# The first load of all on the second DMA queue: k's first head pair issued by ScalarE beside q's first half on SyncE

## The chip, the cores and the metric

One core of a Trainium2 chip. The metric is the device time of one execution in microseconds (us); the median of several executions is quoted. The profile's span, from the first to the last instruction, is some 1.8 us shorter than the time and is used for comparing traces. Runs are compared only with the other kernel's runs from the same rounds on the same chip.

## The reference, cut to what matters

```python
# q, k, v: (8 batches, 8 heads, 576 positions, 64), float32
q_s = softmax(q, axis=-1); k_s = softmax(k, axis=2)
kv  = einsum('bhsd,bhse->bhde', k_s, v)
x   = einsum('bhsd,bhde->bhse', q_s, kv)     # -> (4608 tokens, 512)
h   = x @ w_in                               # w_in (512, 2048)
out = gelu(h) @ w_out                        # w_out (2048, 512), float32
```

## The kernel before

All inputs come in over SyncE's DMA queue, in the order in which the front of the kernel uses them. ScalarE's queue only sends four "touches", loads of 16 x 2 numbers, one from each tensor that is read later. The parts that the argument needs:

```python
    def load_main(b, name, t, parts=1):        # q: 128 partitions x 8 heads
        ...
        for i in range(parts):
            nc.sync.dma_start(out=f[:, i * n:(i + 1) * n, :], in_=src[:, i * n:(i + 1) * n, :])

    def load_pair(b, name, t, parts=1):        # k, v: 128 partitions x 4 head pairs
        ...
        for i in range(parts):
            nc.sync.dma_start(out=f[:, i * n:(i + 1) * n, :], in_=src[:, i * n:(i + 1) * n, :])
    ...
    touch = singles.tile([16, 4, 2], FP32)
    for i, a in enumerate((k[0]..., v[0]..., moe_w_in[0:128:8, 0:2], moe_w_out[0:512:32, 0:2])):
        nc.scalar.dma_start(out=touch[:, i, :], in_=a)

    load_main(0, "q", q, 2)                    # two halves, 524 KB each
    load_pair(0, "k", k, 2)                    # two halves, 590 KB each
    load_pair(0, "v", v, 4)
    wi = [load_wi(i) for i in range(5)]        # w_in in five column blocks
    wo = [load_wo(i) for i in range(3)]
    ...
    exp_q(0, parts=2); exp_k(0, parts=2)       # ScalarE
    norm_q(0, 0, 2)                            # sum on VectorE, product on GpSimd
    norm_q(0, 1, 2, nc.vector)
    tp_mm(0, 0); tp_evac(0, 0, "s")            # transposes of q, copy on ScalarE
    ...
    cast_wi(0, wi[0], "p"); cast_wi(1, wi[1], "p")   # first weight blocks, GpSimd
    ...
    h_phase(0, {...})                          # 64 matmuls with w_in: "the phase"
```

Below, "the phase" is this first matmul phase, and "the gate" is the wait in its middle for w_in's fourth column block.

The softmax here doesn't subtract the row's maximum and nothing guards it: scores larger than these inputs give would overflow.

## Time and profile before

| | before |
|---|---|
| time, median of 3 first runs (range) | 280.57 us (280.5 to 281.31) |
| profiled run: time, span | 280.69, 278.9 us |
| the phase starts | 14.57 us |
| the gate: last piece of w_in's fourth block lands | 21.67 us |
| from the phase's end on | tensor engine without a break |

The prediction shows the chain of waits, the weight loads and the transfers. Some more lines of the kernel before will be needed. The first four are from the timelines by engine (start us, length us, instruction, in brackets the idle time before it and who ended it): q's first exp on ScalarE, GpSimd's casts of v and of the first weight block, and the last weight loads of the tensor engine before the phase, for the small matmuls that multiply q by k.v (kvc).

```profile
4.43 2.62 ACT L133 ACTIVATE e<-f 128x512 bf16<-128x512 f32 x6 [0.30 <-DMA f<-in_q_dram]
...
10.96 2.15 POOL L145 CAST v_aug<-f 128x576 bf16<-128x576 f32 x3 [1.69 <-DMA f<-in_v_dram]
...
13.78 2.59 POOL L378 CAST wi_bf<-w 128x512 bf16<-128x512 f32 x4 [0.68 <-DMA w<-in_moe_w_in_dram]
...
14.23 0.11 PEld L254 LDWEIGHTS <-kvc 64*64 64x64 bf16 x4 [0.71 <-DVE kvc L177]
```

The phase's first weight load at 14.57 comes 0.34 us after the last group of kvc loads begins, at 14.23. The view in the prediction names the weight cast on GpSimd as what ended its wait of 0.23 us. That is an inference from the last signal before it: the first part of that cast had ended at 14.43, and the same 0.34 and 0.23 us stand in the changed kernel, where no cast is named. So the phase did not wait for the weights here; it followed the k.v work, and that waited for GpSimd's last cast of v (end at 13.11, the next k.v weight load at 13.16). The other lines are stretches of the front (from:to, length, busy time of each engine, then clock, DMA share, GB/s):

```profile
1.80:2.80 1.00, 1.00 (x2) 0.48 (x2) 0.14 (x2) 0.17 (x1) 0.00 (x0) 1.00 0.59 151
2.80:5.00 2.20, 2.20 (x3) 0.68 (x3) 0.00 (x0) 1.89 (x4) 0.00 (x0) 1.00 1.09 379
5.00:6.00 1.00, 1.00 (x3) 0.46 (x2) 0.30 (x1) 0.86 (x4) 0.00 (x0) 1.00 1.00 303
6.00:8.00 2.00, 2.00 (x5) 0.87 (x4) 1.97 (x3) 1.05 (x3) 0.64 (x1) 1.00 1.04 366
```

The last column shows the ramp (151) and the dip at the change from q to k (303).

### The profile page before, as it was taken

Reading aid. Unit: us, or ns where it says so; the run is one execution under the profiler, and the core shown is the slowest. Engines: PE = TensorE matmul, PEld = TensorE weight load, DVE = VectorE, ACT = ScalarE, POOL = GpSimd, SP = SyncE. Lnnn points to the kernel's source line nnn. Section 1 sums busy time; section 2 is a strip of 40 time slices with the busy share of each in tenths; the row PEclk is TensorE's granted clock in tenths of the full one; section 3 lists DMA queues with packets and bytes.
Section 4 is the critical chain, followed back from the end, with each engine's and each line's share of the span. In section 5 each row is a group of like instructions: output and inputs, shape, how many; then the busy total and the mean of one; then the engine's idle time right before and its main releaser. Section 6 shows DMA issues by size and latency. Waiting matters only on the chain.

```text
span 278.9 us, 4564 instructions
## 1 busy us (share of the span) xinstructions
PE 272.2 (98%) x1922; PEld 125.8 (45%) x1922; DVE 102.1 (37%) x152; ACT 157.0 (56%) x243; POOL 33.0 (12%) x25
## 2 busy tenths in 40 slices
PE   7899999999999999999999999999999999999995
PEld 3343454444444444444444444444444444444443
DVE  3767486309753530093007500651015200130012
ACT  5747665689377816691569346943683263036400
POOL 1530050002020130004000500050005000000000
PEclk9999999999999999999999999999999999999999
DMA  7999999962993139812981189117501500120033
GB/s 237 385 405 428 399 401 407 399 257 74 305 352 64 41 109 240 329 38 73 256 349 41 40 219 384 49 66 185 119 0 75 150 2 0 75 78 0 0 78 76
DMA packets 44996, 50.10 MB, mean 180 GB/s; under 512 B 20400, under 2 KB 29872, under 8 KB 44720
## 3 DMA queue, kind: packets, MB, share of 16 engines
q1 hardware_dynamic: 44688, 49.68, 53.3%
q8 instruction: 15, 0.25, 0.3%
q10 hardware_dynamic: 288, 0.13, 0.2%
q14 instruction: 5, 0.04, 0.1%
HBM read 36.70 MB, written 9.44 MB: 165 GB/s over the span
## 4 chain that ended last, share of the span: by engine, by line
PE 91%; DMA 7%; DVE 1%; ACTq 0%; issue 0%
PE ps L308 44%; PE ps L298 42%; DMA w<-in_moe_w_in_dram 3%; DMA f<-in_v_dram 2%; PE kv L166 2%; DMA touch<-in_moe_w_in_dram 2%; PE ps L254 1%; PE ps L330 1%; DVE wi_bf L381 0%; ACTq L433 0%; PE ps L259 0%; PE ps L215 0%; PE tp L215 0%; DVE y_sb L335 0%; PE xx L254 0%
## 5 line engine op out<-in xcount | busy, mean ns | idle before, releaser
L298 PE MATMUL ps<-xT,wi_bf 128*128 128x512 bf16 x576 | 126.4, 379 | 0.3
L308 PE MATMUL ps<-wo_bf,g 128*128 128x512 bf16 x560 | 124.2, 379 | 0.0
L303 ACT ACTIVATE g<-ps 128x512 bf16<-128x512 f32 x144 | 85.2, 597 | 69.3 <-PE ps L298 69.3
L298 PEld LDWEIGHTS <-wi_bf 128*128 128x128 bf16 x576 | 56.2, 98 | 68.9 <-DVE wi_bf L381 1.0
L308 PEld LDWEIGHTS <-g 128*128 128x128 bf16 x560 | 53.9, 98 | 64.6 <-issue 0.8
L315 DVE COPY y_sb<-ps 128x512 f32<-128x512 f32 x35 | 23.9, 686 | 81.4 <-PE ps L308 81.1
L198 POOL TENSOR_TENSOR e<-e,recq 128x2048 bf16<-128x2048 bf16 (+1 forms) x9 | 25.7, 2856 | 178.1 <-DVE recq L197 150.0
L145 DVE CAST v_aug<-f 128x576 bf16<-128x576 f32 x26 | 17.9, 745 | 46.9 <-DMA f<-in_v_dram 46.9
L196 DVE TENSOR_REDUCE qsum<-e 128x16 f32<-128x1024 bf16 (+1 forms) x13 | 21.0, 1615 | 13.9 <-ACT e L133 13.9
L280 ACT CAST xT<-ps 128x512 bf16<-128x512 f32 x19 | 10.3, 589 | 26.7 <-PE ps L254 17.1
L133 ACT ACTIVATE e<-f 128x512 bf16<-128x512 f32 (+1 forms) x42 | 20.5, 556 | 2.4 <-DMA f<-in_q_dram 2.0
L138 ACT ACTIVATE ek<-f 128x2304 bf16<-128x2304 f32 (+1 forms) x10 | 17.2, 1730 | 1.8 <-DMA f<-in_k_dram 1.8
L278 DVE CAST xT<-ps 128x512 bf16<-128x512 f32 x15 | 9.7, 687 | 17.5 <-PE ps L254 14.6
L79 ACT ACT_TABLE_LOAD x9 | 11.5, 1283 | 2.8 <-issue 2.6
L415 PE MATMUL ps<-zeros 128*128 128x512 f32 (+1 forms) x14 | 8.6, 764 | 1.5 <-DVE zeros L447 1.5
L133 ACT ACT_TABLE_LOAD x7 | 9.0, 1283 | 0.1
L381 DVE CAST wi_bf<-w 128x512 bf16<-128x512 f32 x12 | 7.4, 661 | 2.6 <-DMA w<-in_moe_w_in_dram 2.3
L166 PEld LDWEIGHTS <-ek 64*64 64x64 bf16 x576 | 6.3, 105 | 2.6 <-issue 1.1
L166 PE MATMUL kv<-v_aug,ek 64*64 64x65 bf16 x576 | 6.9, 193 | 0.0
L198 DVE TENSOR_TENSOR e<-e,recq 128x1024 bf16<-128x1024 bf16 x4 | 6.4, 1606 | 0.1
L254 PE MATMUL ps<-qT,kvc 64*64 64x512 bf16 x60 | 5.0, 390 | 1.0 <-DVE kvc L177 1.0
L408 DVE CAST wo_bf<-w 128x2048 bf16<-128x2048 f32 (+1 forms) x4 | 4.4, 1090 | 3.9 <-DMA w<-in_moe_w_out_dram 3.9
(35 smaller groups left out, 42.8 us busy)
## 6 DMA issues: line engine op xcount, KB each, us to landing
out_dram<-y_sb SPq DMA_DIRECT2D x32, 256.0 KB, 2.3
f<-in_k_dram SPq DMA_DIRECT2D x6, 1152.0 KB, 10.0
f<-in_v_dram SPq DMA_DIRECT2D x6, 1152.0 KB, 11.7
f<-in_q_dram SPq DMA_DIRECT2D x6, 1024.0 KB, 7.1
w<-in_moe_w_in_dram SPq DMA_DIRECT2D x6, 512.0 KB, 8.9
f<-in_k_dram SPq DMA_DIRECT2D x4, 576.0 KB, 10.0
f<-in_v_dram SPq DMA_DIRECT2D x8, 288.0 KB, 7.8
f<-in_q_dram SPq DMA_DIRECT2D x4, 512.0 KB, 8.5
```

What stands on the lines that cost most here:

```text
L79: nc.scalar.activation(out=scr[:, 1:2], in_=scr[:, 0:1], func=func)
L133: nc.scalar.activation(out=dst[:, i], in_=src[:, u], func=AF.Exp)
L138: nc.scalar.activation(out=ek[b % 2][:, i:i + n], in_=st[b]["kf"][:, i:i + n].rearrange("p x (n d) -> p x n d", n=NS), func=AF.Exp,)
L145: eng.tensor_copy(out=v_aug[b % 2][:, hp, :, 0:D], in_=st[b]["vf"][:, hp, :].rearrange("p (n d) -> p n d", n=NS),)
L166: nc.tensor.matmul(ps[c, i, half, 0:D + 1], ek[b % 2][pr, hp, n, :], v_aug[b % 2][pr, hp, n, 0:D + 1], start=(n == 0), stop=(n == NS - 1),)
L196: nc.vector.reduce_sum(out=qsum, in_=eq[:, :, hs, :], axis=AX.X)
L198: eng.tensor_tensor(out=eq[:, :, hs, :], in0=eq[:, :, hs, :], in1=recq.unsqueeze(3).to_broadcast([128, J, w, D]), op=ALU.mult,)
L280: nc.scalar.copy(out=st[b]["xT"][:, hp, :], in_=ps)
L298: nc.tensor.matmul(ps, wi_bf[:, dm, t * 128:(t + 1) * 128], xT[:, dm, :], start=(dm == 0), stop=(dm == NDM - 1),)
L303: nc.scalar.activation(out=g[:, t, :], in_=ps, func=AF.Gelu)
L308: nc.tensor.matmul(ps, st[c]["g"][:, t, j * 128:(j + 1) * 128], wo_bf[:, t, :], start=(t == 0), stop=(t == NDF - 1),)
L315: nc.vector.tensor_copy(out=y_sb, in_=ps)
```

## The change

The intent: no data move before about 1.8 us and the transfers then start slowly, on one queue. k's first head pair (295 KB) goes onto ScalarE's idle queue, in the slot of the touch of k, so that two queues feed the engines from the start. The other touches stay.

```diff
         for i in range(parts):
-            nc.sync.dma_start(out=f[:, i * n:(i + 1) * n, :], in_=src[:, i * n:(i + 1) * n, :])
+            h0 = i * n
+            if b == 0 and name == "k" and i == 0:
+                nc.scalar.dma_start(out=f[:, 0, :], in_=src[:, 0, :])
+                h0 = 1
+            nc.sync.dma_start(out=f[:, h0:(i + 1) * n, :], in_=src[:, h0:(i + 1) * n, :])
...
+    load_main(0, "q", q, 2)
+    load_pair(0, "k", k, 2)
-    touch = singles.tile([16, 4, 2], FP32)
-    for i, a in enumerate((k[0]..., v[0]..., moe_w_in..., moe_w_out...)):
+    touch = singles.tile([16, 3, 2], FP32)
+    for i, a in enumerate((v[0]..., moe_w_in..., moe_w_out...)):
         nc.scalar.dma_start(out=touch[:, i, :], in_=a)
-    load_main(0, "q", q, 2)
-    load_pair(0, "k", k, 2)
```

More of the change, by code (lines that the diff above doesn't have):

```diff
@@ L425, in warm_x @@
                 )
-    touch = singles.tile([16, 4, 2], FP32)
-    for i, a in enumerate((k[0].rearrange("h (p n) d -> (h p) (n d)", n=NS)[0:128:8, 0:2],
-                           v[0].rearrange("h (p n) d -> (h p) (n d)", n=NS)[0:128:8, 0:2],
+    load_main(0, "q", q, 2)
+    load_pair(0, "k", k, 2)
+    touch = singles.tile([16, 3, 2], FP32)
+    for i, a in enumerate((v[0].rearrange("h (p n) d -> (h p) (n d)", n=NS)[0:128:8, 0:2],
                            moe_w_in[0:128:8, 0:2], moe_w_out[0:512:32, 0:2])):
         nc.scalar.dma_start(out=touch[:, i, :], in_=a)
-    load_main(0, "q", q, 2)
-    load_pair(0, "k", k, 2)
     load_pair(0, "v", v, 4)
```

## The prediction

> **What bounds the kernel now.** I read four views of the kernel before, in this order: the page (who is busy), the chain of waits in order of time for the first 60 us (what sets the end), the transfers from 1.2 to 9.2 us in forty slices (what the first loads do), and the timeline of the first 31 us by engine (who waits for which load).
>
> The page first: engine busy times, then the shares of the chain that ended last.
>
> ```profile
> span 278.9 us, 4564 instructions
> PE 272.2 (98%) x1922; PEld 125.8 (45%) x1922; DVE 102.1 (37%) x152; ACT 157.0 (56%) x243; POOL 33.0 (12%) x25
> ...
> PE 91%; DMA 7%; DVE 1%; ACTq 0%; issue 0%
> ```
>
> The tensor engine is the bound. Only 7% of the chain, some 20 us, is transfers, and they are all at the start. So a change to the first load can act on that part alone. The chain there, in order of time (start us, length us, what):
>
> ```profile
> 1.68 4.27 DMA touch<-in_moe_w_in_dram
> ...
> 5.97 6.41 DMA f<-in_v_dram
> ...
> 12.40 9.27 DMA w<-in_moe_w_in_dram
> ...
> 21.69 1.16 DVE wi_bf L381 x2
> 22.89 6.43 PE ps L298 x29
> 29.33 10.36 PE ps L308 x48
> ```
>
> The last transfer on the chain is a piece of the first weight (its fourth block, columns 1024 to 1535, second half). It lands at 12.40 + 9.27 = 21.67 us. Two VectorE casts take it to 22.85, and from 22.89 the tensor engine follows without a break that matters: 48 matmuls in 10.36 us is 0.216 us each. Before that it had started the big matmul phase at 14.57 us. The phase has 64 matmuls, so 64 x 0.216 = 13.8 us of work, and it ends at 29.33: about 0.9 us lie idle in it by the chain. The timeline of the weight loads says where (start, length, what, the wait before and its releaser):
>
> ```profile
> 14.57 4.00 PEld L298 LDWEIGHTS <-wi_bf 128*128 128x128 bf16 x20 [0.23 <-POOL wi_bf L378]
> ...
> 22.36 0.10 PEld L298 LDWEIGHTS <-wi_bf 128*128 128x128 bf16 x1 [0.58 <-DVE wi_bf L381]
> 22.89 5.94 PEld L298 LDWEIGHTS <-wi_bf 128*128 128x128 bf16 x29 [0.43 <-DVE wi_bf L381]
> ```
>
> By 22.36 it has done 34 matmuls, 14.57 + 34 x 0.216 = 21.91; it resumes fully at 22.89 after the 35th. So the loss at this gate is about 22.89 - 21.91 - 0.22 = 0.76 us. That is the model I use: the end moves with the later of two lines, A = start of the phase + 13.8, B = landing of that weight piece + casts + 29 matmuls. Today B is later by about 0.76 us.
>
> What sets that landing? The transfers from 1.2 us on, each slice 0.2 us:
>
> ```profile
> DMA  0003735999999999999998879999999899899999
> GB/s 0 0 0 52 82 113 195 312 374 394 374 364 374 364 374 404 379 364 399 331 339 292 265 288 369 369 357 380 369 380 380 311 346 403 334 357 369 415 392 438
> ```
>
> From 2.8 us the 16 DMA engines are full, and by the slices of the whole page they stay so to beyond 40 us. Each weight piece lies some 9 us in the queue, so its landing is (bytes ahead) / (rate) + (when the stream got going). Only the last is open to this change. Two holes are to be had. The ramp from 1.8 to 2.8 us: the five slices are short of 374 by 322 + 292 + 261 + 179 + 62 = 1116, x 0.2 us = 223 KB, or 0.60 us at 374 GB/s. The dip where q gives way to k (5.0 to 6.0 us): 43 + 35 + 82 + 109 + 86 = 355, x 0.2 = 71 KB, or 0.19 us. Nothing moves before 1.8 us though the first issue is at 0.73, and the change can't help that. So the most that can be won is about 0.8 us, 0.3% of the span.
>
> **What the Trainium skill says.** "DMA: Bandwidth & Descriptors", section "Issuing engines are not separate DMA queues": DMAs started from ScalarE and SyncE run on the same 16 engines and interleave, and a second issuer saves only the sequencer's time. The trace agrees on the steady part: 0.9 to 1.0 busy from 2.8 us with one issuer. Only the ramp, 0.1 to 0.7 busy, leaves anything. Same page, "Queues, rings and completion order": each DMA engine takes turns between queues at packet granularity, a packet being some descriptors. The four tiny touches on ScalarE's queue show a coarse turn here: issued 0.46 us apart (0.74, 1.22, 1.68, 2.16), they land 2.2, 3.3, 4.3 and 5.4 us later, that is at 2.9, 4.5, 6.0 and 7.6, 1.5 us apart. A half of q, 524 KB at 374 GB/s, is 1.4 us. So it looks as if each touch waits for about one whole transfer of the other queue. Same page, "Specifications": a first byte takes about 0.6 us from the sync/scalar path. Here the first packets come at 1.8, 1.1 us after the first issue; the measurement decides.
>
> **The change, part by part.**
>
> Removed: the touch of k, 0.44 us of ScalarE's queue and a few bytes. In its slot ScalarE issues k's first head pair, 128 x 576 floats = 295 KB. One issue costs about as much (0.33 to 0.65 us for the like-shaped v pieces), so the three other touches, the table load (2.63) and the first exp keep their places: zero to +0.2 us, and that exp waits for q anyway.
>
> Moved: SyncE loads k's second head pair alone, so it has one issue more, about 0.4 us. The queue is six microseconds deep there; not on the path. Total bytes are unchanged.
>
> The ramp: two queues now feed the engines from 1.8 us. If the slow start is each queue's own (its first descriptors and first reads), the second stream fills the engines while the first is still slow: up to 0.60 us of the ramp. If it is a slowness of the engines or the memory, nothing. The touch of k did get its 28 packets through by 2.2 us beside q, so the second queue can be served then. I take 0.3 us, half the ramp: my choice, not a reading. For the dip at k I take a quarter, 0.05 us, as k's tensor is now in use before. Sum: landings about 0.35 us earlier all along.
>
> q's cost: 295 KB now compete with q's first half. At 374 GB/s that is 0.79 us, less the 0.3 filled: q's first half lands up to 0.5 us later (4.4 to 4.9), its second half too if the pair is served ahead of it. ScalarE's six exps (4.43 to 7.05) and VectorE's unbroken run from 5.70 (sum, reciprocal, sum, reciprocal, product, cast of v until 11.01) slip by up to 0.5. But k.v needs also the second v cast, on GpSimd, which waits for v until 10.96 and ends at 11.63: 0.6 us of slack against VectorE's 11.01. The transposes of q's second half, ahead of it in the tensor engine's order, slip from 10.5 to about 11.0. So A starts 0 to 0.3 us later (14.57 to 14.87 at worst), while v's and the weights' earlier landings pull the other way. A has 0.76 of slack.
>
> k's first exp needs both head pairs of its half, thus the same bytes as before: 8.05 becomes about 7.7.
>
> Result: B gains 0.35, A is no hindrance: 280.57 - 0.35 = 280.2 us.
>
> **The rivals.**
>
> One, no gain (280.5): the engines serve q's descriptors first and the pair just stands in line, so the ramp stays as it was. For it: the coarse turns seen with the touches, and the skill's sentence on issuers. Against: the early packets of k's touch.
>
> Two, the semaphores bite (280.8 to 281.5). Each load waits for the one eight places before it: v's first piece waited for the touch of k, landed at 2.9, and was issued at 2.98. It now waits for the 295 KB pair, some 4 to 5 us. The touches lie behind the pair, so v's third and fourth pieces and the second weight block, which wait for them, are issued up to 1 us later, at about 6, 7 and 8.5 us. Does the stream run dry? q and k are 2.2 MB; with 0.15 MB gone by 2.8 us they last to 2.8 + 2.05 / 0.374 = 8.3 us, and v's first pieces are then issued since 5. The stock holds. A later touch could also fail to do whatever it was put there for; the touch of v at 5 to 6.5 still precedes v's first packets at about 8.
>
> Three, the late q wins over the early weights (+0.2): it needs A to slip by more than 0.76 us, more than the 0.5 that bytes can give.
>
> Four, the full ramp and dip are won: -0.8, 279.8.
>
> **Range and chances.** Centre 280.2. The three runs before lie at 280.5, 280.57 and 281.31, so chance alone moves a median by a few tenths. From rival four to a no-gain run with some bad luck: 279.7 to 280.9. A 2% change is 5.6 us; the holes hold 0.8 us, and the losses that I can think of under 2. So 1% faster, 98% same, 1% slower.
>
> **What would show it.** Right: slices from 1.8 to 2.8 us nearer to full; 0.3 MB on the second queue there; q's first exp up to 0.5 us later than 4.43; the weight gate at about 21.3 in place of 21.67, and VectorE waits before the weight loads down from 1.0 to some 0.7 us; from there on the same tensor engine work. Wrong: the ramp as before (rival one); DMA slices under 0.9 between 6 and 10 us, or the chain of waits going through a late touch to a late v (rival two); weight loads running unbroken at 22 us but starting much later than 14.57 (rival three).

## The result, and the profile after

The changed kernel takes 280.46 us (median of 6 runs, 280.38 to 280.63); the kernel before took 280.53 in the same rounds (6 runs, 280.42 to 281.31). The ratio is 0.9992, 95% interval 0.9979 to 1.0005: the same. (A ratio is the mean time of one kernel's runs over that of the other's in the same rounds, so not quite the ratio of the medians.) What differs more is the scatter: 0.25 us after, 0.9 us before.

The page of the changed kernel, span and shares of the chain:

```profile
span 278.6 us, 4537 instructions
...
PE 93%; DMA 2%; ACT 1%; issue 1%; DVE 1%; POOL 1%; POOLq 0%
```

Transfers fell from 7% of the chain to 2%, and the span only from 278.9 to 278.6. So something else has taken their place. The chain of waits of the changed kernel, in order of time, names it:

```profile
0.73 4.34 DMA f<-in_q_dram
...
5.10 1.25 ACT e L138 x3
...
6.37 1.23 DVE qsum L201
...
8.03 1.91 POOL e L203
...
11.68 1.28 ACT L79
...
15.38 3.83 PE ps L303 x17
19.25 7.07 PE ps L303 x32
```

No weight is on it any more. It begins with the load of q, which lands at 0.73 + 4.34 = 5.07, and goes through the exp and the sum, later through the small matmuls of k.v and of q with k.v, to the start of the phase. Then the matmuls run through. Its steps from GpSimd's product to the table load (L79) are again inferred, and the last of them is not a wait: in the kernel before, the matmul that is said to follow it began at 12.75, with the table's first use only ending at 13.10. What carries q's delay on is VectorE, which ends the product of q's second half at 11.02, 0.67 us later than before (10.35); the table at the end of the experiments tests that. Weight loads of the tensor engine, to be laid beside those of before:

```profile
14.93 4.00 PEld L303 LDWEIGHTS <-wi_bf 128*128 128x128 bf16 x20 [0.23 <-issue]
19.25 9.38 PEld L303 LDWEIGHTS <-wi_bf 128*128 128x128 bf16 x44 [0.32 <-issue]
```

The waits of 0.58 and 0.43 us at the gate are gone (the block's last piece now lands at 20.94, 0.74 us earlier), and 44 loads run in one piece. But the phase starts at 14.93 in place of 14.57. The timelines say why (ScalarE, VectorE's product, GpSimd's casts, the last kvc loads):

```profile
5.10 1.24 ACT L138 ACTIVATE e<-f 128x512 bf16<-128x512 f32 x3 [0.97 <-DMA f<-in_q_dram]
6.66 1.24 ACT L138 ACTIVATE e<-f 128x512 bf16<-128x512 f32 x3 [0.32 <-DMA f<-in_q_dram]
...
9.47 1.54 DVE L203 TENSOR_TENSOR e<-e,recq 128x1024 bf16<-128x1024 bf16 x1
...
10.35 2.40 POOL L150 CAST v_aug<-f 128x576 bf16<-128x576 f32 x3 [0.42 <-DMA f<-in_v_dram]
...
13.16 2.58 POOL L383 CAST wi_bf<-w 128x512 bf16<-128x512 f32 x4 [0.40 <-DMA w<-in_moe_w_in_dram]
...
14.59 0.11 PEld L259 LDWEIGHTS <-kvc 64*64 64x64 bf16 x4 [0.73 <-DVE kvc L182]
```

GpSimd's last cast of v ends 0.35 us earlier (12.76, was 13.11), and the first weight block is cast 0.62 us earlier (13.16, was 13.78), but q's first exp comes 0.67 us later (5.10, was 4.43). The net of the two traces, counted at the next phase's first weight load: 28.95 before, 28.74 after, 0.2 us, and that difference is still there at the end. The stretches of the front, changed kernel:

```profile
1.80:2.80 1.00, 1.00 (x2) 0.48 (x2) 0.13 (x2) 0.17 (x1) 0.00 (x0) 1.00 0.91 238
2.80:5.00 2.20, 2.20 (x3) 0.68 (x3) 0.00 (x0) 1.31 (x2) 0.00 (x0) 1.00 1.02 351
5.00:6.00 1.00, 1.00 (x3) 0.53 (x2) 0.00 (x0) 0.90 (x3) 0.00 (x0) 1.00 1.07 376
6.00:8.00 2.00, 2.00 (x5) 0.57 (x3) 1.54 (x3) 1.68 (x6) 0.00 (x0) 1.00 1.05 407
```

The same as forty slices of 0.2 us from 1.2 to 9.2 us, to be laid beside the row in the prediction:

```profile
DMA  0006993977999999999999999999999999999999
GB/s 0 0 0 219 300 224 108 339 246 278 371 364 389 394 384 364 359 364 353 384 369 358 376 392 397 403 369 415 403 438 403 392 415 438 415 369 403 438 426 392
```

The ramp is uneven now (DMA 0.91 busy, yet at 238 GB/s), and from 3.2 us no dip is left. In the ramp 87 KB more were moved, but by 5 us 62 KB of them were given back (351 for 379 GB/s, over 2.2 us): 25 KB, or 0.07 us. The gain came later: 73 KB in the dip, 82 KB from 6 to 8 us, together 155 KB, or 0.41 us at 374 GB/s.

### The profile page after: what moved, and what is told of

It reads as the page before. It is cut to its first block, busy times and chain, and to the rows that moved or that the text cites. A ratio compares the mean times of both kernels' runs of the same rounds, so it can differ in the third digit from the quotient of the medians.

```text
span 278.6 us, 4537 instructions
## 1 busy us (share of the span) xinstructions
PE 268.5 (96%) x1894; PEld 125.5 (45%) x1922; DVE 101.7 (36%) x152; ACT 156.7 (56%) x243; POOL 33.2 (12%) x25
## 4 chain that ended last, share of the span: by engine, by line
PE 93%; DMA 2%; ACT 1%; issue 1%; DVE 1%; POOL 1%; POOLq 0%
PE ps L303 45%; PE ps L313 43%; PE kv L171 2%; PE ps L259 2%; DMA f<-in_q_dram 2%; PE ps L335 1%; POOL e L203 1%; ACT L79 0%; ACT e L138 0%; DVE qsum L201 0%; PE ps L220 0%; ACT qT L231 0%; PE ps L264 0%; PE tp L220 0%; DVE kvc L182 0%
## 5 line engine op out<-in xcount | busy, mean ns | idle before, releaser
L313 PE MATMUL ps<-wo_bf,g 128*128 128x512 bf16 x542 | 122.1, 379 | 1.7 <-issue 1.1
L420 PE MATMUL ps<-zeros 128*128 128x512 f32 (+1 forms) x14 | 7.8, 698 | 1.4 <-DVE zeros L451 1.4
```

What stands on the lines that cost most here:

```text
L313: nc.tensor.matmul(ps, st[c]["g"][:, t, j * 128:(j + 1) * 128], wo_bf[:, t, :], start=(t == 0), stop=(t == NDF - 1),)
```

## The experiments

Theory at the outset: the phase starts with the later of two arrivals, q's or the first weights', and runs on with the later of its own work and the gate. The change moved weights and gate forward and q back. (The experiments were read with this theory; its weights turned out to stand for v, as the table at their end shows.) Rivals: a new semaphore order, the dropped touch of k, chance. Each time is a median; "before" in the same rounds was 280.44 (first eight, in two sets on two chips) or 280.33 (last four, on a third chip), 11 runs in each set. All results were correct. Except for the changed kernel and the one before, each rests on a single profile.

**again: the changed kernel once more.**

> The changed kernel unchanged, as a yardstick on this chip. Theory (the weight gate came 0.74 us earlier, 21.67 to 20.94, but the start of the big matmul phase slipped by 0.37 us, 14.57 to 14.94, and is now the bound): the same two numbers within 0.1 us, time 0.1 to 0.3 us under before. Rival (the two traces differ by chance): gate or start off by more than 0.2 us from those.

280.51 us (5 runs, 280.33 to 280.53), ratio 0.9999 (0.9988 to 1.0011). Phase start 15.03, and the gate's piece at 20.86: as before it within 0.1. The time was level with the kernel before, not 0.1 to 0.3 under it. On this chip the runs of before scattered from 280.15 to 281.04. So the change, on the mean, wins nothing, and the 0.2 us between the first two traces needed a second look (b1, b2).

**e1_order: the reordering alone.**

```diff
+    load_main(0, "q", q, 2)
+    load_pair(0, "k", k, 2)                 # all on SyncE
+    touch = singles.tile([16, 3, 2], FP32)  # v, w_in, w_out
```

> Only the reordering: touch of k dropped, the other touches after the k loads, all of k on SyncE. Theory (the gain in the stream comes from the second queue's bulk bytes in the ramp): slices of the ramp as before, q's first exp at 4.4, gate at 21.5 to 21.8, phase start 14.5 to 14.7, time equal to before within 0.15 us. Rival (the dropped touch or the new semaphore order frees the stream): gate at 21.0 to 21.2, and as q is not delayed, time 0.4 us or more under before.

280.86 us, ratio 1.0011 (0.9999 to 1.0023). q's first exp at 4.49, first weight cast at 14.10, start at 14.87. The dropped touch and the new order do not free the stream. The expectation of the gate was missed: the piece landed at 20.88, even before the rival's 21.0 to 21.2, and there was no wait at it in this profile (weight loads unbroken from 19.19), though v and the first weights had come no earlier than before. And it lost some 0.4 us at 43 us, where batch 1's loads are used. That pointed at chance in single transfers.

**e2_qsplit: the second queue carries half of q's first half, k stays on SyncE.**

```diff
+            if b == 0 and i == 0:
+                nc.scalar.dma_start(out=f[:, 2:4, :], in_=src[:, 2:4, :])
+                nc.sync.dma_start(out=f[:, 0:2, :], in_=src[:, 0:2, :])
+                continue
```

> The bytes on the second queue are q's own: heads 0 and 1 of the first half on SyncE, heads 2 and 3 on ScalarE, k on SyncE as before, touches as in the changed kernel. Theory (the ramp is filled by any bulk on the second queue, and what cost the gain was q's first half delayed by k's bytes): q's first exp at 3.9 to 4.4 in place of 5.10, phase start 14.2 to 14.5, gate at 20.9 to 21.2, time 0.5 us or more under before. Rival (ramp gain needs k's tensor, or the phase start is not set by q): gate or start as in before or the changed kernel, time within 0.2 us of one of them.

280.87 us, ratio 1.0012 (1.0000 to 1.0024). q was served earlier (exp at 4.22), as expected, but the start was 14.93, and 0.41 us of waiting was left at the gate: the first weight cast began only at 14.20. The rival holds in one part: q's own bulk on the second queue doesn't bring the stream forward.

**e3_qhalf: q's whole second half on the second queue.**

```diff
+            eng = nc.scalar if b == 0 and i == 1 else nc.sync
```

> More bytes beside q's first half: q's whole second half (524 KB in place of 295 KB) on ScalarE. Theory (q's first half waits for the bytes beside it, and the phase start follows from q): first exp at 5.3 to 5.9, phase start at 15.0 to 15.6, gate at 20.9 to 21.2 all the same, time 0.1 to 0.6 us over the changed kernel. Rival (the end follows the gate, not the phase start): time as the changed kernel within 0.1 us. With q's second half arriving first, the exp of it would follow at once, which could make up part.

280.88 us, ratio 1.0021 (1.0005 to 1.0037). Exp at 5.45, start at 15.28, no wait at the gate; 0.4 us over the changed kernel (one run of six, 281.97, at a granted clock of 0.994: the share of the tensor engine's full clock that it was given). q's delay passes to the start one for one: exp 5.10, 5.21, 5.45 and start 14.93, 15.03, 15.28. That the time follows the start, not the gate, held.

**b1 and b2: the kernel before, profiled again.**

> The kernel before, unchanged, for a second profile of it and its own scatter. Theory (its end hangs on a lottery: the fourth weight block is held up by the one DMA engine, of sixteen, that fetches 16 KB of instructions at 17 us, if that engine is among the last): this profile shows either the gate as before (a wait for casts at 22.4 and 22.9) with a span of 278.8 to 279.2, or no gate at all and a span of 278.3 to 278.6. Phase start at 14.5 to 14.9 in either. Rival (the spread of its times, 280.15 to 281.04, comes from later in the kernel or from the clock): the tensor engine's times at 29 us do not go with the span.

> A third profile of the kernel before, to be read as b1: gate with a longer span, or no gate with a shorter one.

b1: 280.35 us (6 runs, 280.23 to 281.03), ratio 0.9998 (0.9986 to 1.0010), profiled run 280.75. b2: one run, 280.46. Weight cast and weight loads of b1:

```profile
14.45 2.58 POOL L378 CAST wi_bf<-w 128x512 bf16<-128x512 f32 x4 [0.68 <-DMA w<-in_moe_w_in_dram]
...
15.24 4.00 PEld L298 LDWEIGHTS <-wi_bf 128*128 128x128 bf16 x20 [0.23 <-POOL wi_bf L378]
19.56 9.38 PEld L298 LDWEIGHTS <-wi_bf 128*128 128x128 bf16 x44 [0.32 <-issue]
```

My form of the lottery theory was missed by b1: no wait at the gate, but a long span (279.0), because the start itself had come 0.67 us later than in the first profile. The chain of b1 shows through what:

```profile
4.54 7.06 DMA f<-in_v_dram
...
11.65 0.67 POOL v_aug L145
...
13.85 0.48 PE kv L166 x36
...
14.90 0.41 PE ps L254 x4
15.31 4.21 PE ps L298 x19
```

It goes through v, its cast and k.v, and no weight is on it; so do the chains of b2 and e2. In b2 the cast of the weights came at 14.08, the start at 14.87, and a gate wait of 0.41 us was left. So the kernel before has two throws, as of dice: when v and behind it the first weight block land (weight cast at 13.78, 14.08, 14.45), and whether the gate holds (its piece at 21.67, 21.48, 21.09 in before, b2, b1). Its first profile had the best start of the three and the worst gate.

The trace's completion counts show the first throw. Each load runs on 16 DMA engines, and counts as landed when the last is through. For the first weight block, with the landing of v's last piece beside it (us):

| | first engine | eighth | last | last - first | v's last piece, last engine |
|---|---|---|---|---|---|
| before | 12.96 | 13.17 | 13.73 | 0.78 | 12.38 |
| b2 | 12.72 | 13.08 | 14.03 | 1.31 | 12.68 |
| b1 | 12.87 | 13.25 | 14.40 | 1.53 | 13.06 |
| after | 12.46 | 12.69 | 13.11 | 0.65 | 11.69 |
| again | 12.66 | 12.82 | 13.03 | 0.36 | 11.61 |

With the change the eighth engine is ahead by some 0.4 us and the engines are closer together. The second throw: in the run of again, fifteen engines finished the gate's piece by 19.51 and the last at 20.86, and one engine had first fallen back between the loads that ended at 16.96 and 19.62; in the first profile of before it was 20.20 and 21.67. In both, one packet of 16 KB on the queue for instructions was under way just then (from 17.21 in again and from 16.87 in before, 0.93 us long). That a fetch of instructions holds up one of the 16 engines fits both traces; the counts don't name the engine and no run removed the fetch, so it is not shown.

**e4_touch: q split as in e2, touch of k put back.**

```diff
+                tk = singles.tile([16, 2], FP32, name="tk")
+                nc.sync.dma_start(out=tk, in_=k[0]...[0:128:8, 0:2])
```

> q's first half split over both queues as in e2, but with the touch of k put back (on SyncE, right after q's first two heads). Theory (what spoilt e2 and e1 was the dropped touch of k: some DMA engines lose up to 0.5 to 1 us at k's first bytes and lag from then on): k's first exp at 7.7 to 8.1 in place of e2's 8.45, first v piece at 10.0 to 10.2 in place of 10.63, phase start 14.1 to 14.5, time 0.3 to 0.6 us under e2. Rival (the touch does nothing; e2's late k is chance or queue order): k and v as in e2, time as e2.

283.34 us, ratio 1.0100 (1.0082 to 1.0118): far off both, and five of the six runs had a granted clock of 0.994 or 0.988. The experiment is spoilt. Every packet of the load queue took longer: between 9 and 40 us the median is 49 ns for 1024 bytes (46 in the changed kernel), 87 for 2048 (84), 164 for 4096 (159). In the built program the small tile that I had added moved all load tiles by 32 bytes, from address 75520, a multiple of 256, to 75552. e8 has the same tile, the same shift and the same packet times; none of the other profiles has. Besides, q's second half, behind the touch, was late (exp at 7.69). The touch is left open.

**e5_half: half of the pair.**

```diff
-                nc.scalar.dma_start(out=f[:, 0, :], in_=src[:, 0, :])
+                w = NS * D // 2
+                nc.scalar.dma_start(out=f[:, 0, 0:w], in_=src[:, 0, 0:w])
+                nc.sync.dma_start(out=f[:, 0, w:], in_=src[:, 0, w:])
```

> Half the bytes of the change on ScalarE (first 288 columns of k's first head pair, 147 KB; the other half on SyncE). Theory (q's delay is set by the bytes beside it): q's first exp at 4.7 to 4.9, about half of the 0.67 us, phase start 14.6 to 14.8, k still warmed early, so stream near that of the changed kernel (first v piece 9.6 to 9.9), time 0.0 to 0.3 us under the changed kernel. Rival (the delay of q is a fixed cost of the second queue being busy): exp at 5.1, start at 14.9.

280.44 us (280.41 to 280.51), ratio 0.9997 (0.9985 to 1.0009), so equal to the changed kernel. ScalarE's timeline:

```profile
5.14 1.24 ACT L140 ACTIVATE e<-f 128x512 bf16<-128x512 f32 x3 [1.03 <-DMA f<-in_q_dram]
```

The rival holds: with half the bytes q is just as late. The trace's packets say how. In the changed kernel no packet of q moved before 2.25 us, and one or so per engine by 2.75, while the pair's went; in the kernel before q's began after 1.75. Here the second queue's load takes the slow start, and q has its own behind it: q reaches 90 packets in a quarter of a microsecond from 2.75 us in before, from 3.5 in the changed kernel and in e5. The weights did not clearly come forward (cast at 13.92, and 13.78 to 14.45 in the kernel before).

**e6_vpair: v's first head pair in the pair's place, k on SyncE with its touch.**

```diff
-            if b == 0 and name == "k" and i == 0:
+            if b == 0 and name == "v" and i == 0:
```

> The same 295 KB on ScalarE's queue, but of v (its first head pair), k whole on SyncE with its touch. Theory (the stream's gain came from k's first bytes being read in the ramp: the dip where q gives way to k is gone, not the ramp filled): q's first exp at 5.0 to 5.3 as in the changed kernel, but the dip stays (two or more slices under 320 GB/s between 5 and 6.5 us) and the first weight block's cast starts at 13.7 to 14.4, as before; phase start 15.0; time 0.0 to 0.3 us over the changed kernel. Rival (any bulk on the second queue from a new tensor): no dip, first weight cast at 13.0 to 13.3 as in the changed kernel.

Three runs at full clock took 280.38, 280.74 and 280.91 us; three had a granted clock of 0.994 and took 281.40 to 281.97 (so had one of the eleven of the kernel before, with 282.83). Median 281.15, ratio 1.0020 (0.9990 to 1.0050). Exp at 4.97, start at 14.81. The cast came at 13.61, between the two theories, and the dip was one slice of 312 GB/s, where two under 320 were expected to stay. Undecided: k's pair did better than v's, but v's wasn't without effect.

**e7_qk: q split over both queues, k's pair second on ScalarE.**

```diff
+                nc.scalar.dma_start(out=f[:, 2:4, :], in_=src[:, 2:4, :])   # q, first on ScalarE
+                nc.sync.dma_start(out=f[:, 0:2, :], in_=src[:, 0:2, :])
...                                                  # k's pair follows; no touch of w_out
```

> A try to keep both: q's first half split over the two queues as in e2, k's first head pair behind it on ScalarE (touch of w_out dropped). Theory (start of phase is the later of q's first exp + 9.83 and first weight cast + 0.79): exp at 4.2 to 4.4, first weight cast at 13.1 to 13.6, start at 14.1 to 14.5 unless q's second half, now behind k, takes over (its exp at 6.3 to 6.7, start then 14.6 to 14.8). Time 0.1 to 0.5 us under the changed kernel. Rival (k's early bytes help only when they come before q): weight cast at 13.9 or later, start 14.7 or later, no gain.

280.51 us, ratio 0.9998 (0.9968 to 1.0029). Exp at 4.23 and weight cast at 13.08: both as good as hoped. But q's second half now waits (exp at 6.81), and in two of six runs the granted clock was lower (0.994). One stretch of the profiled run, which is one of those two:

```profile
10.00:16.00 6.00, 4.37 (x96) 2.30 (x96) 3.05 (x8) 3.61 (x6) 4.71 (x7) 0.72 1.07 390
```

The clock was 0.72 on the mean from 10 to 16 us, and the phase started at 15.87. The four runs at full clock took 280.21 to 280.51, the two slower ones 281.29 and 281.37. The best time is no better than the best of before (280.08), so this is no version that beats both.

**e8_second: touch of k first, then the pair.**

```diff
+                nc.scalar.dma_start(out=tk, in_=k[0]...[0:128:8, 0:2])
                 nc.scalar.dma_start(out=f[:, 0, :], in_=src[:, 0, :])
```

> As the changed kernel, with the touch of k put ahead of the pair on ScalarE's queue, so that the pair is issued at 1.21 in place of 0.74 us (touch of w_out dropped). Theory (an engine serves whichever queue's transfer came first, whole): q's first half goes first on most engines, first exp at 4.4 to 4.6, second half's at 6.4 to 6.7. Start between 14.3 and 14.8, time 0.1 to 0.4 us under the changed kernel. Rival (ScalarE's queue is preferred whatever the order): exp at 5.1, start 14.9.

282.04 us, ratio 1.0049 (1.0021 to 1.0076), spoilt by the same 32-byte shift as e4. Exp at 4.94 and 7.29, start at 15.24. Neither expectation holds, and nothing is concluded from the time; the ends of q and v before its start are used below.

**e9_double: both head pairs of k's first half.**

```diff
-                nc.scalar.dma_start(out=f[:, 0, :], in_=src[:, 0, :])
-                h0 = 1
+                nc.scalar.dma_start(out=f[:, 0:2, :], in_=src[:, 0:2, :])
+                continue
```

> Twice the bytes: both head pairs of k's first half (590 KB) on ScalarE in one load. Theory (q waits until the second queue's transfer is through; the slow start costs about the same for 147 and 295 KB, further bytes come at the full rate): q's first exp at 5.6 to 6.0 (5.15 + 295 KB at 374 GB/s = 0.79), start at exp + 9.83 = 15.4 to 15.8, time 0.5 to 0.9 us over the changed kernel. Rival (engines alternate by packets, q only shares): exp at 5.1 to 5.4, start 15.0 to 15.2.

282.92 us, ratio 1.0073 (1.0043 to 1.0103); at full clock 281.83 and 281.86. ScalarE's timeline:

```profile
4.76 0.20 ACT L79 ACTIVATE scr<-scr 128x1 f32<-128x1 f32 x1
6.36 1.24 ACT L138 ACTIVATE e<-f 128x512 bf16<-128x512 f32 x3 [1.40 <-DMA f<-in_q_dram]
```

q came at 6.36, later even than the 5.6 to 6.0 of the theory, and two runs at full clock lost 1.4 us against the changed kernel. From 3.75 to 4.75 us the trace has 25 to 29 packets of k (2304 bytes, one row each) and 25 to 28 of q (1024 bytes) in each quarter of a microsecond: the two queues move equal numbers of rows here, and as k's rows are longer, q gets under a third of the bytes. Part of the rival, taking turns, is so; its conclusion, that q is hardly delayed, is not. The phase started at 17.49, with the clock at half from 12 to 14 us.

In e9 q's packets moved first (from 1.87 us, k's from 2.70), in the changed kernel k's did (from 1.81, q's from 2.32). The traces tell the two apart by a small thing: which of the two issuing instructions ended first. SyncE's ended at 1.19 or 1.20 us in every profile. ScalarE's ended at 1.16 or 1.17 in after, again, e5 and e6, and there ScalarE's load moved first; it ended at 1.22 to 1.24 in e2, e3, e4, e7 and e9, and there SyncE's load moved first. In all nine the other queue's rows began 0.3 to 1.0 us later. No run set this order on purpose, so it is a rule that fits and not one that was tested.

**What the starts say together.** Two ends explain the start of the phase: q's, the end of VectorE's product of q's second half, and v's, the end of GpSimd's last cast of v. Take the later of q's end + 3.91 and v's end + 1.46 (the two offsets are those of the first traces, after and before; the sums are of unrounded times):

| | q's end | v's end | q's end + 3.91 | v's end + 1.46 | start |
|---|---|---|---|---|---|
| before | 10.35 | 13.11 | 14.26 | 14.57 | 14.57 |
| b2 | 10.40 | 13.40 | 14.32 | 14.86 | 14.87 |
| b1 | 10.46 | 13.78 | 14.38 | 15.24 | 15.24 |
| e1_order | 10.41 | 13.41 | 14.32 | 14.88 | 14.87 |
| e2_qsplit | 10.12 | 13.47 | 14.03 | 14.93 | 14.93 |
| after | 11.02 | 12.76 | 14.93 | 14.22 | 14.93 |
| again | 11.12 | 12.87 | 15.04 | 14.33 | 15.03 |
| e5_half | 11.06 | 13.24 | 14.98 | 14.71 | 14.97 |
| e3_qhalf | 11.37 | 13.11 | 15.28 | 14.57 | 15.28 |
| e6_vpair | 10.89 | 12.91 | 14.81 | 14.37 | 14.81 |
| e8_second | 11.33 | 13.21 | 15.24 | 14.67 | 15.24 |

Eleven profiles, within 0.01 us. The kernels of the upper five rows wait for v, those of the lower six for q. A first form of the rule (q's first exp + 9.83, first weight cast + 0.79) came within 0.06 us in ten of them, because v and the weights arrive on one stream; it missed e8 by 0.4, where q's second half was late. In all eleven the phase's first load came 0.34 us after the last group of kvc loads had begun, so it never waited for the weights. Of the other three, e4 did wait for them (the first part of the cast ended at 15.91, start 15.97); e7 and e9 start 1.1 and 1.3 us later than the rule says, with the clock at half from 12 to 14 us in both.

## Why the prediction was right or wrong, point by point

The time (280.2 foretold, 280.46 measured) lies in the range, and "same" was right. That is in part luck: the range held a run without any gain as well. The gain of 0.35 us was not there: -0.07 us by the medians, with an interval on both sides of nothing.

- **What bounds the kernel: half right.** The two lines A and B were the right model, and with A binding the phase took 13.81 us from its first weight load to that of the next phase, as worked out. But B was later by less than 0.76 us: the phase took 14.38 us, so 0.57 was lost (of the 0.76, 0.2 was made up after the gate: 29 matmuls in 6.06 us, not 29 x 0.216 = 6.26). And that was one throw of a scattering kernel. In b1 B did not bind at all, and in b2 and b1 A started at 14.87 and 15.24. "A has 0.76 of slack" was the step that failed: there was a slack of 0.57, 0.09 and none in three profiles. What sets A was also missed: the prediction followed v up to the second of its four casts, and the fourth, ending at 13.11, set the start.
- **The ramp, 0.3 us: wrong in size.** It was filled (0.91 busy for 0.59), but net it gave 0.07 us by 5 us.
- **The dip, 0.05 us: wrong in size, the other way.** Dip and the two microseconds after it gave 0.41 us. The weights' landing gained even more, 0.62 to 1.37 us by the five profiles, and the engines stay closer together. Why k's early bytes do that is not settled: k's pair (e7 too) brings the cast to 13.1, v's to 13.6, half a pair to 13.9, each of the last two in one profile; q's bytes alone (e2, e3) leave it at 13.95 to 14.2, and the kernel before had 13.78 to 14.45. The touch stays untested.
- **q's cost, up to 0.5 us: wrong in size.** It was 0.67 and 0.78. I took it as bytes at the full rate. Here it was a place in line: half the bytes cost as much (e5). In e3 and e9, where q moved first, it was shared bytes.
- **A starts 0 to 0.3 us later: nearly.** 0.37 later than the first profile, but that start had followed v, not q. Against the mean of three starts (14.57, 14.87, 15.24: 14.89) the new starts of 14.93 and 15.04 are level. This is where the gain went: v comes earlier, q later, and the start stays.
- **Rival one, no gain:** right in the time, wrong in the reason, for the stream did move. The coarse turns of the touches, on which it leaned, don't hold for bulk loads (e9). **Rival two, semaphores:** v's first piece was issued at 3.91 in place of 2.98, and no harm was seen. **Rival three, late q against early weights:** near to the mechanism that came (v stands in the weights' place), against my "more than the 0.5 that bytes can give". **Rival four:** the gate's landing did gain 0.74 on the first profile, close to the whole 0.8, but only 0.55 and 0.16 on b2 and b1, and it wasn't the end that counted.

The change does one thing the prediction didn't ask about: in these profiles it swaps a bound that scatters (v's end, 13.11 to 13.78) for one that scatters less (q's end, 11.02 and 11.12). Eleven runs of the changed kernel lie between 280.33 and 280.63; the seventeen of before in the same rounds between 280.15 and 281.31. That the times scatter less for this reason fits, but too few runs were profiled to show it. The bound that it gives up was also at times the faster one (lowest 280.15 against 280.33).

## What to carry to other kernels

A transfer put on a second queue at the very start can take the place in line from what was first; if both feed the same start, the question is which of the two arrivals is the later, not how full the engines are. Before a wait of a few tenths in one profile is taken for the gain on offer, profile the same kernel two or three times: a landing waits for the slowest of 16 engines, and that is a throw. A releaser that a view names is inferred: compare the idle time with a profile where it is not named, before a wait is built on it. And when an experiment adds a small tile, look whether it shifts the addresses of the big ones.

## What the Trainium skill lacked or had wrong

- "DMA: Bandwidth & Descriptors", "Issuing engines are not separate DMA queues": it says a second issuer only saves the sequencer's time. Here moving 295 KB to it delayed the first queue's first load by 0.67 us (0.78 in again) and brought a weight block's last engine from 13.73 - 14.40 to 13.03 - 13.11 us. Which queue is served first matters (in nine profiles it was the one whose issue ended first, by 0.02 to 0.05 us), and the page doesn't speak of it.
- The same page, "Queues, rings and completion order": turns are by packets of some 9 to 17 descriptors. In e9, with both queues full, the records show near equal counts of single rows (27 of 2304 bytes and 26 of 1024 bytes in 0.25 us). Equal counts would come of any equal turns, but the number of k's rows in flight does not persist either: from 3.5 to 4.75 us its correlation with itself 46 ns later is 0.0, where turns of nine such rows on 16 engines would give some 0.8 (worked out by a small simulation). If a record is one descriptor, the turns are much shorter than nine.
- No page that I found gives a figure for the spread between the 16 engines of one load: 0.36 to 1.53 us for 524 KB here, nor that one engine alone can fall some 1.4 us behind the fifteenth (20.86 against 19.51 in again), at the time of a fetch of instructions (16 KB, 0.93 us).
- The same page, "How a descriptor splits into AXI transactions", says that a descriptor that starts off a 256-byte boundary costs extra beats, as bytes before its start are fetched and not used, and speaks of reads. Load targets shifted by 32 bytes off it took 49 for 46, 87 for 84 and 164 for 159 ns (1024, 2048 and 4096 bytes): the direction agrees, on the writing side.
